# Attention states kept compact: state product in quarters of the array, state update by heads in column halves, y in two banks shared with the scores

One core of one Trainium2 chip runs the whole program. The metric is device time of one execution in microseconds (us); every time here is the median of a kernel's fast runs if nothing else is said. "TensorE" is the matrix engine, "VectorE" the vector engine, "ScalarE" the one for activation functions, "GpSimd" the general engine, "SyncE" the one that issues most of the transfers.

## What is computed

```python
batch, n_heads, seq, head_dim = (4, 8, 768, 64)
for t in range(S):                                   # retention, per batch and head
    state = gamma * state + outer(k[t], v[t])        # 64 x 64
    y[t] = scale * (q[t] @ state)
x = y.transpose(0, 2, 1, 3).reshape(B * S, H * D)    # 3072 x 512
h = x @ w_in                                         # 512 x 2048
g = h * sigmoid(1.702 * h)
out = g @ w_out                                      # 2048 x 512, fp32
```

The kernel does the recurrence by chunks of 128 tokens: 4 sequences of 6 chunks. In a chunk, y is the masked scores times v (the score part) plus q times the state that the chunk found (the state part); then the state is updated with k and v of the chunk. A sequence's first chunk has no state part and its last no update. Four chunks are one block of 512 tokens for the MLP. The weights come as 8-byte numbers and are narrowed to fp32 by VectorE and ScalarE in the first 155 us or so.

## The kernel before

The attention of a chunk, which runs between units of the MLP's matmuls (cuts are marked `# ...`):

```python
y = ps.tile([P, HP, P], F32, name="py", tag="att")          # one bank; pt and pu use the same two buffers
if c:
    for hp in range(HP):                                    # state part: 2 heads at once, block-diagonal 128x128 state
        pe.matmul(y[:, hp, :], old[:, hp, :], qt[:, hp, :], start=(hp == 0), stop=False, ...)
for hp in range(HP):                                        # score part: column halves
    for i in range(2):
        pe.matmul(y[i * D:(i + 1) * D, hp, :], vn[:, 2 * hp + i, :], a[:, i, hp, :], ...)
dve.tensor_mul(x[...], y, rowd)                             # y read out and scaled
# ...
u = ps.tile([P, HP, P], F32, name="pu", tag="att")
for hp in range(HP):                                        # update: 128x128, of which only two 64x64 corners are wanted
    h = slice(2 * hp, 2 * hp + 2)
    pe.matmul(u[:, hp, :], kd[:, h, :]..., vn[:, h, :]..., start=True, stop=True)
for i in range(2):                                          # the two corners, one after the other
    r = slice(i * D, (i + 1) * D)
    # ...
    pool.tensor_mul(new[r, :, r], old[r, :, r], cold[r, 2 * H:, None]...)
    dve.tensor_add(new[r, :, r], new[r, :, r], u[r, :, r])
```

The fetch of a piece of w_in, and what SyncE's queue holds at the start:

```python
w1v = moe_w_in.bitcast(U32).rearrange("(c p) (f two) -> p c f two", p=P, two=2)
# ...
sp.dma_start(x.rearrange("p (c f) two -> p c f two", c=2) if i < NFF else x, SRC[i])   # 512 KB over 128 partitions
# ...
load(0)                    # q, k, v of the first chunk
fetch()
load(1)                    # q, k, v of the second chunk
for _ in range(5):
    fetch()
# ...
turn(0)                    # transposes q and k; then queues q and k of the third chunk, behind the six fetches
```

Of the kernel before, what the change touches and what calls it, by code (L numbers as in the profile page):

```python
# [9 lines left out]
F32 = mybir.dt.float32  # L10
U32 = mybir.dt.uint32
AF = mybir.ActivationFunctionType
ALU = mybir.AluOpType
P = 128
# [14 lines left out]
def kernel(  # L29
# [29 lines left out]
    pe, act, dve, pool, sp = nc.tensor, nc.scalar, nc.vector, nc.gpsimd, nc.sync  # L59
    ctx.enter_context(tc.manual_schedule(engines={mybir.EngineType.PE}))  # L60

    B, H, S, D = q.shape
    NT, DM = out.shape
    DFF = moe_w_in.shape[1]
    HP = H // 2
# [6 lines left out]
    NFF = DFF // P  # L72
    NP = NFF // 2
# [4 lines left out]
    const = ctx.enter_context(tc.tile_pool(name="const", bufs=1))  # L78
    one = ctx.enter_context(tc.tile_pool(name="one", bufs=1))
    two = ctx.enter_context(tc.tile_pool(name="two", bufs=2))  # L80
    ps_a = ctx.enter_context(tc.tile_pool(name="ps_a", bufs=1, space=bass.MemoryType.PSUM))
    ps = ctx.enter_context(tc.tile_pool(name="ps", bufs=2, space=bass.MemoryType.PSUM))
# [13 lines left out]
    rowd = const.tile([P, HP, P], F32, name="rowd")  # L96
    cold = const.tile([P, 2 * H + HP], F32, name="cold")
    ident = const.tile([P, P], F32, name="ident")
    mask = const.tile([P, 2, HP, P], F32, name="mask")
    state = [const.tile([P, HP, P], F32, name=f"state{i}") for i in range(2)]  # L100


    QKV = {}
# [1 line left out]
    def load(j, what="qkv"):  # L105


        b, c = divmod(j, NC)
        rows = slice(c * P, (c + 1) * P)

        def plain(name, src, tag, bufs):
            QKV[name, j] = two.tile([P, H, D], F32, name=name + "_in", tag=tag, bufs=bufs)
            sp.dma_start(QKV[name, j], src[b, :, rows, :].rearrange("h p d -> p h d"))

        if j < 2 * CB:
            if "q" in what:
                plain("q", q, "q_sq", 2)
                plain("kn", k, "k_sq", 2)
        else:
            for name, src in (("q", q), ("k", k)):  # L120
                t = two.tile([P, HP, P // C4, C4], F32, name=name + "_sq")
                for r0 in range(0, P, C4):
                    d0 = r0 % D
                    for hp in range(HP):
                        tc.keep_in_program_order(sp.dma_start(
                            t[r0:r0 + C4, hp],
                            src[b, 2 * hp + r0 // D, rows, d0:d0 + C4].rearrange("(s p) d -> p s d", p=C4)))
                QKV[name, j] = t
            if c < NC - 1:
                plain("kn", k, "kn", 1)  # L130
        if "v" in what:
            plain("v", v, "v", 2)


    w1v = moe_w_in.bitcast(U32).rearrange("(c p) (f two) -> p c f two", p=P, two=2)
    w2v = moe_w_out.bitcast(U32).rearrange("(f p) (e two) -> p f e two", p=P, two=2)
    RAWS = [r.rearrange("p a b -> p (a b)").bitcast(U32)
            for r in (W2[:, 4], W2[:, 5], G[:, 6:8].rearrange("p a s t -> p a (s t)"))]

    SRC = [w1v[:, 2 * h:2 * h + 2, 2 * p * P:2 * (p + 1) * P] for p in range(NP) for h in range(2)] \  # L140
        + [w2v[:, f] for f in range(NFF)]
    fetched = [0]

    def raw(i, n=1):
        x = RAWS[i // 2 % 3]
        return x[:, i % 2 * 1024:(i % 2 + n) * 1024]

    def fetch():
        i = fetched[0]
        if i < len(SRC):  # L150
            x = raw(i).rearrange("p (n two) -> p n two", two=2)
            sp.dma_start(x.rearrange("p (c f) two -> p c f two", c=2) if i < NFF else x, SRC[i])
            fetched[0] = i + 1

    narrowed = [0]
# [1 line left out]
    def narrow():  # L157


        i = narrowed[0]  # L160
        if i == len(SRC):
            return
# [29 lines left out]
        for _ in range(n):  # L192
            fetch()
# [4 lines left out]
    def home(j, name):  # L198

        at = ["qT", "kT", "kd", "at"].index(name)  # L200
        shape = [[HP, P], [HP, P], [H, D], [2, HP, P]][at]
        if j >= 2 * CB:
            return one.tile([P] + shape, F32, name=name, tag=name)
        if at < 3:
            t = G[:, at, j % 2 * 2:j % 2 * 2 + 2]
            return t.rearrange("p s t -> p (s t)").rearrange("p (a b) -> p a b", a=shape[0])
        return G[:, 3 + j % 2].rearrange("p s t -> p (s t)").rearrange("p (a b c) -> p a b c", a=2, b=HP)
# [19 lines left out]
            load(j + 2, "qk" if j + 2 < 2 * CB else "qkv")  # L227

    def attend(j):
        p = ps_a.tile([P, 2, HP, P], F32, name="pa")  # L230
        for hp in range(HP):
            for i in range(2):
                r = slice(i * D, (i + 1) * D)
                pe.matmul(p[:, i, hp, :], KT[j][r, hp, :], QT[j][r, hp, :], start=True, stop=True)  # L234
        AT[j] = home(j, "at")
        for i in range(2):
            dve.tensor_mul(AT[j][:, i], p[:, i], mask[:, i])  # L237
        KT.pop(j)

    def finish(j):  # L240
        c = j % NC
        old, new = state[c % 2], state[(c + 1) % 2]
        vn, a, qt = QKV.pop(("v", j)), AT.pop(j), QT.pop(j)
        y = ps.tile([P, HP, P], F32, name="py", tag="att")
        if c:
            for hp in range(HP):
                pe.matmul(y[:, hp, :], old[:, hp, :], qt[:, hp, :], start=(hp == 0), stop=False,  # L247
                          skip_group_check=True)
        for hp in range(HP):
            for i in range(2):  # L250
                pe.matmul(y[i * D:(i + 1) * D, hp, :], vn[:, 2 * hp + i, :], a[:, i, hp, :],  # L251
                          start=(not c and hp == 0), stop=(hp == HP - 1), skip_group_check=True)
        half, t0 = divmod(j % CB * P, TH)
        x = X1 if j // CB == 1 else X
        dve.tensor_mul(x[:, 2 * half:2 * half + 2, :, t0:t0 + P].rearrange("p s c t -> p (s c) t"), y, rowd)  # L255
        if j + 2 < 2 * CB:
            load(j + 2, "v")
        if c == NC - 1:
            return
        kd = KD.pop(j)  # L260
        u = ps.tile([P, HP, P], F32, name="pu", tag="att")
        for hp in range(HP):
            h = slice(2 * hp, 2 * hp + 2)
            pe.matmul(u[:, hp, :], kd[:, h, :].rearrange("p i d -> p (i d)"),  # L264
                      vn[:, h, :].rearrange("p i d -> p (i d)"), start=True, stop=True)
        for i in range(2):
            r = slice(i * D, (i + 1) * D)
            if c == 0:
                dve.tensor_copy(new[r, :, r], u[r, :, r])  # L269
            else:  # L270
                pool.tensor_mul(new[r, :, r], old[r, :, r],  # L271
                                cold[r, 2 * H:, None].to_broadcast([D, HP, D]))
                dve.tensor_add(new[r, :, r], new[r, :, r], u[r, :, r])


    def hidden(g, h):
# [156 lines left out]


    act.dma_start(cold, col_decay)
    for s in range(2):
        act.dma_start(
            rowd[s * D:(s + 1) * D],
            bass.AP(tensor=row_decay.tensor, offset=row_decay.offset + s * P,
                    ap=[[0, D], [2 * P, HP], [1, P]]),  # L440
        )
    load(0)
    fetch()
    load(1)
    for _ in range(5):
        fetch()
    make_identity(nc, ident)

    for i in range(2):
        for hp in range(HP):  # L450
            h = 2 * hp + i
# [1 line left out]
    m3 = mask.rearrange("s i h t -> s (i h) t")  # L453
    pool.affine_select(out=m3, in_=m3, compare_op=ALU.is_ge, fill=0.0, base=0,
                       pattern=[[0, H], [1, P]], channel_multiplier=-1)

    for t in state:
        dve.memset(t, 0.0)

    def chunks(m):  # L460

        return [s for j in range(m * CB, (m + 1) * CB)
                for s in (lambda j=j: turn(j), lambda j=j: attend(j), lambda j=j: finish(j))]

    turn(0)
    for j in range(CB):
        attend(j)
        narrow()
        turn(j + 1)
        finish(j)  # L470
        if j == 0:
            narrow()
        else:
            up0(0, j - 1)
# [78 lines left out]
```

## Time and profile before

| | before |
|---|---|
| time | 724.99 us (724.62 to 725.17, 3 runs) |
| TensorE busy | 705.4 us, 98% of the span of 722.5 |
| full chunk of attention in the later part, by differences of starts | 3.00 us |
| first matmul of the second block's up-projection | 114.1 us |

The last row splits the run in two. Before 114.1 the weights arrive and are narrowed, and TensorE waits now and then; after it TensorE is hardly ever idle (busy 603.9 of 608.4 us). The 608.4 us from there to the end of the span can be counted in matmuls, the start can't. TensorE's first 30 us:

```profile
11.22 1.09 PE L217 MATMUL pt<-ident,q_in 128*128 128x128 f32 x4 [0.60 <-DMA q_in<-in_q_dram]
...
21.57 1.09 PE L217 MATMUL pt<-ident,q_in 128*128 128x128 f32 x4 [4.41 <-DMA q_in<-in_q_dram]
```

(start, length, engine, line, operation, result and operands, count; in brackets the idle time ahead and what ended it. Of the results, pt is a transpose, pa the scores, py the chunk's y, pu its update, ph the MLP's up-projection and pd its down-projection; G, W and X are buffers that several things share.)

### The profile page before, as it was taken

What the parts mean: (1) busy time and instruction counts of PE and PEld (TensorE: products, weight loads), DVE (VectorE), ACT (ScalarE), POOL (GpSimd) and SP (SyncE); (2) the same over time, 40 slices, a digit from 0 to 9 for tenths busy, and PEclk for the clock granted to TensorE, in tenths of its full rate; (3) what the DMA queues carried; (4) which work ended last, traced back from release to release, by engine and by line L of the source; (5) the groups of instructions that cost most, each with busy time, mean ns of one, the idle gap of its engine ahead of it and who ended that gap; (6) DMA issues with size and microseconds to landing.
All of it is one profiled execution on the core that took longest, in us unless ns stands there. A gap on an engine that the chain in (4) does not pass through costs nothing.

```text
span 722.5 us, 9662 instructions
## 1 busy us (share of the span) xinstructions
PE 705.4 (98%) x3776; PEld 588.5 (81%) x3776; DVE 373.2 (52%) x542; ACT 126.7 (18%) x197; POOL 125.7 (17%) x115
## 2 busy tenths in 40 slices
PE   5799999999999999999999999999999999999997
PEld 4688885447888888888888888888888888888886
DVE  4888889993612822443743353553345373244251
ACT  2313323221000001331000332000233000133100
POOL 2241001000464403000333000123100140200030
PEclk9899999999999999999999999999999999999999
DMA  9995333420012324101334200324300320100001
GB/s 255 232 199 145 132 132 114 147 35 11 15 45 40 73 49 103 31 1 16 74 59 87 59 1 8 73 46 86 67 0 2 63 54 1 44 0 1 15 0 44
DMA packets 142765, 46.28 MB, mean 64 GB/s; under 512 B 129920, under 2 KB 136576, under 8 KB 142720
## 3 DMA queue, kind: packets, MB, share of 16 engines
q1 hardware_dynamic: 135504, 39.10, 23.8%
q10 hardware_dynamic: 7216, 6.57, 2.9%
q8 instruction: 30, 0.49, 0.3%
q14 instruction: 15, 0.12, 0.1%
HBM read 39.33 MB, written 6.29 MB: 63 GB/s over the span
## 4 chain that ended last, share of the span: by engine, by line
PE 92%; DVE 5%; DMA 1%; ACT 1%; issue 0%; SPq 0%; ACTq 0%
PE pd L403 38%; PE px L352 15%; PE py L352 11%; PE ph L313 8%; PE ph L300 7%; PE py L251 3%; PE pa L234 3%; PE pu L264 3%; PE py L247 2%; DMA q_in<-in_q_dram 1%; PE pt L217 1%; DVE W L342 1%; DVE G L342 1%; DVE W L343 1%; DVE G L343 1%; ACT W L181 0%
## 5 line engine op out<-in xcount | busy, mean ns | idle before, releaser
L403 PE MATMUL pd<-W,G 128*128 128x256 f32 x1120 | 250.3, 381 | 0.4 <-DVE G L343 0.3
L403 PEld LDWEIGHTS pd<-W,G 128*128 128x128 f32 x1120 | 210.1, 190 | 30.8 <-DVE G L343 1.2
L352 PE MATMUL px<-X,W 128*128 128x256 f32 x512 | 119.0, 379 | 0.0
L352 PEld LDWEIGHTS px<-X,W 128*128 128x128 f32 x512 | 97.3, 190 | 13.2
L352 PE MATMUL py<-X,W 128*128 128x256 f32 x384 | 90.7, 379 | 0.0
L352 PEld LDWEIGHTS py<-X,W 128*128 128x128 f32 x384 | 73.0, 190 | 9.9
L300 PE MATMUL ph<-X,W 128*128 128x256 f32 x256 | 58.2, 382 | 0.0
L225 POOL TENSOR_TENSOR kd<-kn_in,cold 128x512 f32<-128x512 f32 x13 | 13.6, 1042 | 242.0 <-PE pu L264 199.0
L313 PE MATMUL ph<-W,W 128*128 128x512 f32 x128 | 55.1, 592 | 0.0
L300 PEld LDWEIGHTS ph<-X,W 128*128 128x128 f32 x256 | 47.5, 190 | 6.7 <-DVE X L255 0.2
L313 PEld LDWEIGHTS ph<-W,W 128*128 128x128 f32 x128 | 24.3, 190 | 30.2 <-issue 29.2
L344 POOL TENSOR_TENSOR G<-G 128x512 f32<-128x512 f32 x20 | 28.9, 1444 | 113.1 <-DVE G L343 111.7
L237 DVE TENSOR_TENSOR at<-pa,mask 128x512 f32<-128x512 f32 x32 | 20.6, 684 | 45.5 <-PE pa L234 45.5
L281 DVE TENSOR_TENSOR G<-G,sg 128x512 f32<-128x512 f32 x48 | 33.0, 688 | 13.7 <-ACT sg L279 13.7
L279 ACT ACTIVATE sg<-G 128x512 f32<-128x512 f32 x48 | 30.3, 630 | 50.9 <-DVE G L362 30.6
L279 ACT ACTIVATE sg<-ph 128x512 f32<-128x512 f32 x32 | 19.1, 598 | 104.7 <-PE ph L300 56.2
L403 PE MATMUL pd<-W,W 128*128 128x256 f32 x160 | 35.6, 380 | 0.4 <-DVE W L343 0.3
L403 PEld LDWEIGHTS pd<-W,W 128*128 128x128 f32 x160 | 30.2, 190 | 5.6 <-DVE W L343 1.2
L271 POOL TENSOR_TENSOR state<-state,cold 64x256 f32<-64x256 f32 x32 | 25.6, 800 | 44.0 <-DVE state L269 24.8
L255 DVE TENSOR_TENSOR X<-py,rowd 128x512 f32<-128x512 f32 x20 | 13.8, 688 | 33.3 <-PE py L251 33.3
L390 ACT ACTIVATE u<-pd 128x512 f32<-128x512 f32 x6 | 3.6, 597 | 155.1 <-PE pd L403 155.1
L362 DVE TENSOR_TENSOR G<-py,p 128x512 f32<-128x512 f32 x16 | 11.1, 691 | 37.8 <-PE py L352 37.8
(96 smaller groups left out, 682.1 us busy)
## 6 DMA issues: line engine op xcount, KB each, us to landing
v_in<-in_v_dram SPq DMA_DIRECT2D x24, 256.0 KB, 3.9
W<-in_moe_w_in_dram SPq DMA_DIRECT2D x12, 512.0 KB, 5.1
out_dram<-o ACTq DMA_DIRECT2D x24, 256.0 KB, 2.4
kn_in<-in_k_dram SPq DMA_DIRECT2D x21, 256.0 KB, 4.1
W<-in_moe_w_out_dram SPq DMA_DIRECT2D x10, 512.0 KB, 3.7
q_sq<-in_q_dram SPq DMA_DIRECT2D x256, 16.0 KB, 1.8
k_sq<-in_k_dram SPq DMA_DIRECT2D x256, 16.0 KB, 1.8
G<-in_moe_w_out_dram SPq DMA_DIRECT2D x6, 512.0 KB, 3.8
```

Source lines behind the costliest of these rows:

```text
L234: pe.matmul(p[:, i, hp, :], KT[j][r, hp, :], QT[j][r, hp, :], start=True, stop=True)
L237: dve.tensor_mul(AT[j][:, i], p[:, i], mask[:, i])
L251: pe.matmul(y[i * D:(i + 1) * D, hp, :], vn[:, 2 * hp + i, :], a[:, i, hp, :], start=(not c and hp == 0), stop=(hp == HP - 1), skip_group_ ...
L264: pe.matmul(u[:, hp, :], kd[:, h, :].rearrange("p i d -> p (i d)"), vn[:, h, :].rearrange("p i d -> p (i d)"), start=True, stop=True)
L271: pool.tensor_mul(new[r, :, r], old[r, :, r], cold[r, 2 * H:, None].to_broadcast([D, HP, D]))
L279: act.activation(s, h, AF.Sigmoid, scale=1.702)
L281: dve.tensor_mul(g, h[:, i], s[:, i])
L300: pe.matmul(h[:, ab], w, X[:, 2 * half + c // 2, c % 2, :], start=(ab == 0 and c == 0), stop=(c == 3), skip_group_check=True)
L313: pe.matmul(h, w, X1[:, c // 2:4:2, c % 2, :], start=(c == 0), stop=(c == 3))
L344: pool.tensor_sub(a[1], a[1], a[0])
L352: pe.matmul(acc[:, u, :], W1[:, 2 * d + u, sa, c, :], X[:, sb, c, :], start=(start and u == 0 and c == 0), stop=(stop and c == 1), skip_gr ...
L403: pe.matmul(p0[:, n, :], g1(m, p, sa)[:, n * P:(n + 1) * P], W2[:, sb, p, :], start=(new and p == 0 and n == 0), stop=(last and p == NP - ...
```

## The change

The state of two heads was a 128x128 block of which two 64x64 corners are used, so TensorE multiplied zeros in the state part and computed unwanted corners in the update. Now the state is 64 columns wide: the state part becomes eight 64x64 products on four quarters of the array, the update eight products on column halves with 64 moving columns, and its VectorE and GpSimd work one instruction each. The new y takes the two banks of the scores, in turn with them, one for each row half. That puts other pairs of heads side by side in x, so w_in's rows are permuted to match as they are fetched. Each 512 KB fetch of w_in thereby becomes two, of 64 partitions each.

```diff
-    state = [const.tile([P, HP, P], F32, ...) for i in range(2)]
+    state = [const.tile([P, HP, D], F32, ...) for i in range(2)]
-    w1v = moe_w_in.bitcast(U32).rearrange("(c p) (f two) -> p c f two", p=P, two=2)
+    w1v = moe_w_in.bitcast(U32).rearrange("(o c r d) (f two) -> c r d o f two", o=2, c=2, d=D, two=2)
# ... fetch:
-            sp.dma_start(x.rearrange("p (c f) two -> p c f two", c=2) if i < NFF else x, SRC[i])
+            if i < NFF:
+                for c in range(2):
+                    sp.dma_start(x[c * D:(c + 1) * D].rearrange("p (o f) two -> p o f two", o=2), SRC[i][c])
+            else:
+                sp.dma_start(x, SRC[i])
# ... finish:
-        y = ps.tile([P, HP, P], F32, name="py", tag="att")
+        y = ps_a.tile([P, 2, HP, P], F32, name="py", tag="pa")
+        where = [(y[s % 2 * D:(s % 2 + 1) * D, r, s // 2, :], s, r) for s in range(HP) for r in range(2)]
         if c:
-            for hp in range(HP):
-                pe.matmul(y[:, hp, :], old[:, hp, :], qt[:, hp, :], ...)
+            for out, s, r in where:
+                k = slice(r * D, (r + 1) * D)
+                pe.matmul(out, old[k, s, :], qt[k, s, :], ...)
+        for out, s, r in where:
+            pe.matmul(out, vn[:, 2 * s + r, :], a[:, r, s, :], ...)
# ... the update:
-        u = ps.tile([P, HP, P], F32, name="pu", tag="att")
+        u = ps.tile([P, HP, D], F32, name="pu", tag="att")
+        for s in range(HP):
+            for r in range(2):
+                pe.matmul(u[r * D:(r + 1) * D, s, :], kd[:, 2 * s + r, :], vn[:, 2 * s + r, :], ...)
+        # ... whole-tile copy, or scale and add, in place of two halves
-    for t in state:
-        dve.memset(t, 0.0)
# ... (row decays loaded in the new order of heads)
```

More of the change, by code (lines that the diff above doesn't have):

```diff
@@ L99 @@
     mask = const.tile([P, 2, HP, P], F32, name="mask")
-    state = [const.tile([P, HP, P], F32, name=f"state{i}") for i in range(2)]
+    state = [const.tile([P, HP, D], F32, name=f"state{i}") for i in range(2)]
     QKV = {}
@@ L138 @@
             for r in (W2[:, 4], W2[:, 5], G[:, 6:8].rearrange("p a s t -> p a (s t)"))]
-    SRC = [w1v[:, 2 * h:2 * h + 2, 2 * p * P:2 * (p + 1) * P] for p in range(NP) for h in range(2)] \
+    SRC = [[w1v[c, h, :, :, 2 * p * P:2 * (p + 1) * P] for c in range(2)] for p in range(NP) for h in range(2)] \
         + [w2v[:, f] for f in range(NFF)]
@@ L229, in attend @@
     def attend(j):
-        p = ps_a.tile([P, 2, HP, P], F32, name="pa")
+        p = ps_a.tile([P, 2, HP, P], F32, name="pa", tag="pa")
         for hp in range(HP):
@@ L243, in finish @@
         vn, a, qt = QKV.pop(("v", j)), AT.pop(j), QT.pop(j)
-        y = ps.tile([P, HP, P], F32, name="py", tag="att")
+        y = ps_a.tile([P, 2, HP, P], F32, name="py", tag="pa")
+        where = [(y[s % 2 * D:(s % 2 + 1) * D, r, s // 2, :], s, r) for s in range(HP) for r in range(2)]
         if c:
-            for hp in range(HP):
-                pe.matmul(y[:, hp, :], old[:, hp, :], qt[:, hp, :], start=(hp == 0), stop=False,
-                          skip_group_check=True)
-        for hp in range(HP):
-            for i in range(2):
-                pe.matmul(y[i * D:(i + 1) * D, hp, :], vn[:, 2 * hp + i, :], a[:, i, hp, :],
-                          start=(not c and hp == 0), stop=(hp == HP - 1), skip_group_check=True)
+            for out, s, r in where:
+                k = slice(r * D, (r + 1) * D)
+                pe.matmul(out, old[k, s, :], qt[k, s, :], start=(s < 2), stop=False, skip_group_check=True)
+        for out, s, r in where:
+            pe.matmul(out, vn[:, 2 * s + r, :], a[:, r, s, :], start=(not c and s < 2), stop=(s >= 2),
+                      skip_group_check=True)
         half, t0 = divmod(j % CB * P, TH)
         x = X1 if j // CB == 1 else X
-        dve.tensor_mul(x[:, 2 * half:2 * half + 2, :, t0:t0 + P].rearrange("p s c t -> p (s c) t"), y, rowd)
+        dve.tensor_mul(x[:, 2 * half:2 * half + 2, :, t0:t0 + P], y[:, :, 0:2, :],
+                       rowd.rearrange("p (r o) t -> p r o t", r=2))
         if j + 2 < 2 * CB:
@@ L260, in finish @@
         kd = KD.pop(j)
-        u = ps.tile([P, HP, P], F32, name="pu", tag="att")
-        for hp in range(HP):
-            h = slice(2 * hp, 2 * hp + 2)
-            pe.matmul(u[:, hp, :], kd[:, h, :].rearrange("p i d -> p (i d)"),
-                      vn[:, h, :].rearrange("p i d -> p (i d)"), start=True, stop=True)
-        for i in range(2):
-            r = slice(i * D, (i + 1) * D)
-            if c == 0:
-                dve.tensor_copy(new[r, :, r], u[r, :, r])
-            else:
-                pool.tensor_mul(new[r, :, r], old[r, :, r],
-                                cold[r, 2 * H:, None].to_broadcast([D, HP, D]))
-                dve.tensor_add(new[r, :, r], new[r, :, r], u[r, :, r])
+        u = ps.tile([P, HP, D], F32, name="pu", tag="att")
+        for s in range(HP):
+            for r in range(2):
+                pe.matmul(u[r * D:(r + 1) * D, s, :], kd[:, 2 * s + r, :], vn[:, 2 * s + r, :],
+                          start=(s == 0), stop=True, skip_group_check=True)
+        if c == 0:
+            dve.tensor_copy(new, u)
+        else:
+            pool.tensor_mul(new, old, cold[:, 2 * H:, None].to_broadcast([P, HP, D]))
+            dve.tensor_add(new, new, u)
     def hidden(g, h):
@@ L435 @@
     act.dma_start(cold, col_decay)
-    for s in range(2):
-        act.dma_start(
-            rowd[s * D:(s + 1) * D],
-            bass.AP(tensor=row_decay.tensor, offset=row_decay.offset + s * P,
-                    ap=[[0, D], [2 * P, HP], [1, P]]),
-        )
+    for c in range(2):
+        for r in range(2):
+            act.dma_start(
+                rowd[c * D:(c + 1) * D, 2 * r:2 * r + 2],
+                bass.AP(tensor=row_decay.tensor, offset=row_decay.offset + (2 * c + r) * P,
+                        ap=[[0, D], [4 * P, 2], [1, P]]))
     load(0)
```

## The prediction

> **What bounds the kernel now.** I read the page's busy line and slices first, then the chain that ended last, then one attention chunk in the timeline, then stretches of the start.
>
> ```profile
> PE 705.4 (98%) x3776; PEld 588.5 (81%) x3776; DVE 373.2 (52%) x542; ACT 126.7 (18%) x197; POOL 125.7 (17%) x115
> PE   5799999999999999999999999999999999999997
> DVE  4888889993612822443743353553345373244251
> PE 92%; DVE 5%; DMA 1%; ACT 1%; issue 0%; SPq 0%; ACTq 0%
> PE pd L403 38%; PE px L352 15%; PE py L352 11%; PE ph L313 8%; PE ph L300 7%; PE py L251 3%; PE pa L234 3%; PE pu L264 3%; PE py L247 2%; DMA q_in<-in_q_dram 1%; PE pt L217 1%; DVE W L342 1%; DVE G L342 1%; DVE W L343 1%; DVE G L343 1%; ACT W L181 0%
> ```
>
> TensorE is the bound: 98% busy, all but a few us of its idle time in the first two slices. The changed lines are on the chain with 2% (L247, queries times state), 3% (L251, values times scores) and 3% (L264, the update): about 58 us at most, so only a shorter TensorE program gains. The second row to watch is VectorE, at eight to nine tenths in the first nine slices. A steady chunk (times are starts):
>
> ```profile
> 239.94 1.16 PE L234 MATMUL pa<-qT,kT 64*128 64x128 f32 x16
> ...
> 241.03 3.72 PE L403 MATMUL pd<-W,G 128*128 128x256 f32 x16
> ...
> 243.50 1.28 DVE L237 TENSOR_TENSOR at<-pa,mask 128x512 f32<-128x512 f32 x2
> ...
> 244.59 1.05 PE L247 MATMUL py<-qT,state 128*128 128x128 f32 x8
> ...
> 245.57 1.09 PE L251 MATMUL py<-at,v_in 128*64 128x128 f32 x16
> ...
> 246.59 1.16 PE L264 MATMUL pu<-v_in,kd 128*128 128x128 f32 x8
> ...
> 247.59 2.76 PE L403 MATMUL pd<-W,G 128*128 128x256 f32 x12
> ...
> 249.85 0.68 DVE L255 TENSOR_TENSOR X<-py,rowd 128x512 f32<-128x512 f32 x1
> ```
>
> Every fp32 matmul shows as two records (L247's four as x8), so two passes. Differences of the starts are what TensorE spends: 0.98 us on the state part of y, 1.02 on the score part, 1.00 on the update, 3.00 for a chunk with all three. The state and update matmuls run on the whole array (128*128), the score part in column halves (128*64).
>
> [...]The 16 pd records between pa and L247 take 3.56 us, where the chain gives 16 records without a switch 3.45, so 0.11 is a weight load laid bare. The 32 pd records that run into the next pa take 254.59-247.59 = 7.00 where the chain has 6.91, so 0.09 is the drain. One switch is 0.20 us into 128 columns, about 0.15 into 64. [...]L247 less its drain is 0.89 us for 8 records, 0.112 each. Half-array records run in pairs: the 16 of L251, less 0.09 drain and 0.05 load, take 0.88, so 8 slots of 0.109. [...]
>
> **The change part by part.**
> State part of y: four whole-array matmuls become eight 64x64 ones. They write 16 records, each streaming 128 columns as before, on four tiles. Four at a time is 4 slots of 0.109 = 0.44 us in place of 0.89. It adds a switch before it (0.09 drain; its own load is 0.05) and the one after it now leads from quarters to halves.
> Score part: the same 16 records in 8 slots, 0.88 + 0.05 load. The order is now four passes of one half, then four of the other, where it was two and two.
> Update: four whole-array matmuls become eight column halves with 64 moving columns. [...]So 16 records in 8 slots of about 0.056 are 0.45, for 0.89. It follows the score part in the same mode, so the switch between them (0.20) goes. One is added behind it, back to pd (0.20).
> Sum for a chunk with all three: before 3.00; after 0.09 + (0.05+0.44+0.09) + (0.05+0.88) + 0.45 + (0.09+0.11) = 2.25. Saved 0.75. A sequence's first chunk has no state part: before 0.09+1.02+1.00 = 2.11, after 0.09+0.93+0.45+0.20 = 1.67, saved 0.45 with rounding. Its last has no update: 2.11 against 1.80, saved 0.31. With 4 sequences of 6 chunks: 16 x 0.75 + 4 x 0.45 + 4 x 0.31 = **15.0 us** if nothing waits. Of it 5.0 belong to the eight chunks of the first 115 us, 10.0 to the sixteen after.
>
> What takes some back: y now shares its two banks with the scores. So its first matmul waits until VectorE has read both halves of the scores; before, only the score part needed them, 0.98 us later. In the chunk above the reading ends at 243.50+1.28 = 244.78, 0.19 after y starts at 244.59. Less the 0.09 of drain[...], the wait is about 0.16. The same place in each of the four later blocks (the chunk that meets the sums on VectorE) has this, the other twelve have 2.2 us of slack: -0.65 in all. The other direction is free there: X<-py ends at 250.53, the next scores start at 254.59.
>
> In the start it costs more. Comparing the reading's end with y's start for chunks 2 to 7, chunks 2, 3, 5 and 7 have y 0.13, 0.37, 0.70 and 0.47 ahead of it, so waits of about 0.3, 0.5, 0.7 and 0.4. Chunk 0 gains nothing (TensorE waits for q until 21.6 anyway), chunk 1 part of it:
>
> ```profile
> 20.00:30.00 10.00, 7.92 (x43) 6.38 (x44) 9.25 (x13) 3.40 (x4) 2.02 (x2) 0.66 0.95 214
> 40.00:50.00 10.00, 9.69 (x78) 8.24 (x77) 9.84 (x13) 2.75 (x4) 4.24 (x4) 1.00 0.86 206
> 90.00:114.00 24.00, 24.00 (x158) 21.05 (x155) 21.98 (x31) 5.84 (x9) 3.85 (x4) 1.00 0.34 110
> ```
>
> (columns: PE, PEld, DVE, ACT, POOL busy us with counts, clock, DMA share, GB/s). With VectorE at 9.25, 9.84 of 10 and 21.98 of 24 us, and DMA at 0.95, TensorE can't run far ahead. Of the 5.0 us I keep 2.
>
> Off the path: the state updates on 64x256 halves (VectorE about 0.42 us, twice a chunk) become one on 128x256, so VectorE loses some 0.4 us a chunk, and GpSimd half its state instructions; both only help the start. The two memsets (0.5 us each) lay before the first data. The q and k transposes no longer share their two buffers with y; that removes waits of 0.3 to 0.5 us of L247 on ScalarE in chunks 1 to 3, which the new wait replaces. Sixteen w_in fetches become thirty-two of half size, and SyncE needs some 0.4 us for each more, on a stretch where DMA is full: up to 0.5 us lost.
>
> Net: 10.0 - 0.65 + 2 - 0.5 = about 11 us, if the array packs as hoped.
>
> **The rivals.**
> (a) Quarters don't run four at a time, only two. For: nothing in this trace shows more than two tiles at once, and two passes of one tile stand next to each other. Against: pairs already overtake a waiting pass[...]. Then the state part is 0.88 instead of 0.44, costing 0.44 x 20 = 8.8 us: about 722.5.
> (b) The new order of the score part, four passes of one half in a row, is longer than the look-ahead. One slot lost per chunk is 0.109 x 24 = 2.6 us, two 5.2. For: no place in the trace has such a run. Against: in pairs the second tile starts as if the first's queue were not there. About 716.5 to 719.
> (c) The new wait on VectorE eats all the start's gain and more: the start then gives 0, about 716.
> (d) Everything packs and the start gains its whole 5 us, as VectorE is relieved: about 711.
>
> **Range and chances.** Full packing gives 725.0 - 11 = 714. I give (a) one in six, some of (b) one in three, and (d) one in five; these about cancel around the middle, so I say 714.0 us, with 709.5 to 721 to hold it 8 times in 10. A gain over 2% needs 14.5 us, nearly all of the 15.0 without a wait: 0.15. Slower by 2% would need the change to cost more than every gain, and I see no wait of that size: 0.02. The rest, 0.83, is within 2%.
>
> **What would show it right or wrong.** In the timeline of a late chunk: the state part's 16 records 0.58 us from the first start to the score part's (1.0 means rival a); the score part to the update 0.93 (1.04 or more means b); the update to pd about 0.54. A full chunk is 2.25 us instead of 3.00. TensorE idle before the state part, put down to VectorE's scores line, should be 0.1 to 0.2 us in four late chunks and 0.3 to 0.7 in some early ones. The third part, the up-projection of the second block, should start about 2 us before its 114.1. I am wrong if the late chunks save nothing, or if the first 115 us grow.

What is cut from this text are rules and figures that no trace of this case shows: on changes of shape, on weight loads, on the order of matmuls, on banks, on the split of a transfer, on tiles, and an allowance of time for VectorE's signal. Its sum came to 10.0 - 0.65 + 2 - 0.5 = about 11 us. The 0.65 is four waits of 0.16, of which 0.19 - 0.09 = 0.10 each comes from the trace and the rest is the allowance. The 0.5 for the split fetch stands on SyncE's records (q's at 0.80 and 20.07 us take 0.44 and 0.42); that the halves themselves would be no slower was not measured.

"Drain" and "load" are names for times that the trace of before shows at a change of shape; what the array does in them it doesn't show. Within L247's run and within L251's, a pass follows on the one before it (in L251 a pair on a pair) after 0.11 us. Into the score part it is 0.20 (245.37, 245.57), so 0.09 more, and to its second pair 0.16 (245.73), so 0.05 more; into the update it is 0.20 (246.39, 246.59) and to its second pass 0.21 (246.81), 0.10 more. The weight loads' records take 190 ns for 128 columns (update) and 136 for 64 (score part). The slot of 0.056 in the update is an estimate, half of the 0.112 between L247's records. "Look-ahead" is the word for how many waiting passes of one tile a pass of another can overtake. That they overtake is in the trace: all of L251's 16 records start in pairs less than 0.01 us apart, the first pair included (245.57, 245.58), though the program has the two passes of one half next to each other.

## More of the kernel before

TensorE transposes the second chunk's q at 11.22 and the third chunk's at 21.57, and waits 4.41 us for the latter to arrive. What the transfers do meanwhile, by stretches:

```profile
12.00:16.00 4.00, 3.90 (x30) 3.01 (x28) 3.28 (x6) 1.87 (x3) 1.04 (x1) 1.00 1.05 362
16.00:20.00 4.00, 1.17 (x17) 0.97 (x16) 3.86 (x8) 0.00 (x0) 2.04 (x2) 1.00 1.10 357
```

(busy us and counts of TensorE, its weight loads, VectorE, ScalarE, GpSimd; granted clock; share of the DMA engines; GB/s moved.) The last two columns count: the DMA engines are full, and while w_in's rows of 2 KB arrive, full means some 360 GB/s. (In the 4 us before, which bring mostly the short rows of q, k and v, they are as full and move 254.)

## The result

The changed kernel takes 719.56 us (718.91 to 720.40, 4 runs) where the kernel before took 725.08 beside it (4 runs): ratio 0.9919, 95% interval 0.9899 to 0.9940, so some 5.9 us faster. Ratios here are the mean time of one kernel's fast runs over that of the other's of the same rounds, so they differ a little from the ratio of the medians. A second submission of the same file gave 0.9909 (0.9895 to 0.9923).

The changed kernel's busy times and its first slices:

```profile
PE 693.1 (97%) x4096; PEld 572.5 (80%) x4096; DVE 362.6 (51%) x520; ACT 126.8 (18%) x197; POOL 111.2 (15%) x99
...
PE   5599999999999999999999999999999999999997
...
DVE  2787898995512742444643444463345373244251
```

TensorE is busy 12.3 us less than before, but the span shrank by only 4.8 (722.5 to 717.7): the rest became idle time. The second slice of TensorE fell from 7 to 5, and VectorE's first slices from 4, 8, 8, 8, 8 to 2, 7, 8, 7, 8. Nearly all of that is in the start. A late chunk of the changed kernel, the counterpart of the chunk in the prediction (one of the four in which VectorE is busy with sums for the MLP):

```profile
243.26 3.72 PE L408 MATMUL pd<-W,G 128*128 128x256 f32 x16
247.16 0.67 PE L256 MATMUL py<-qT,state 64*64 64x128 f32 x16 [0.18 <-DVE at L242]
247.75 1.15 PE L258 MATMUL py<-at,v_in 128*64 128x128 f32 x16
248.68 0.69 PE L272 MATMUL pu<-v_in,kd 128*64 128x64 f32 x16
249.29 0.92 PE L408 MATMUL pd<-W,G 128*128 128x256 f32 x3
```

By differences of starts the state part takes 0.60 us instead of 0.98, the score part 0.92 instead of 1.02, the update 0.61 instead of 1.00: four 64x64 tiles do run at once (in this chunk four of the state part's records start within 0.02 us, from 247.155 to 247.175). From the first pd record ahead of it to the state part it is 3.90 here, against 3.65 in a chunk without a wait, so the new wait on VectorE costs 0.25, of which the trace shows 0.18 as idle. The start, in contrast:

```profile
12.30 1.09 PE L222 MATMUL pt<-ident,q_in 128*128 128x128 f32 x4 [2.37 <-DMA q_in<-in_q_dram]
...
27.08 1.12 PE L222 MATMUL pt<-ident,q_in 128*128 128x128 f32 x4 [8.29 <-DMA q_in<-in_q_dram]
```

The third chunk's q is there 5.5 us later than before; TensorE waits 8.29 us for it instead of 4.41. The stretches show why: the DMA engines are as full as before and move a third less.

```profile
12.00:16.00 4.00, 3.58 (x22) 2.92 (x24) 1.29 (x3) 1.19 (x2) 1.04 (x1) 1.00 1.14 227
16.00:20.00 4.00, 2.77 (x38) 2.42 (x34) 3.38 (x7) 0.67 (x1) 0.99 (x1) 1.00 1.07 242
```

In the trace of before, whole 512 KB fetches land 1.40 us apart (14.64, 16.10, 17.44, 18.81, 20.23 us); in the changed kernel halves land 1.08 apart (16.09, 17.17, 18.25, 19.33), so 2.16 for the same bytes. Six fetches lie ahead of the third chunk's q: 6 x 0.76 = 4.6 of the 5.5 us.

The late arrival goes with a lower clock, too. The third number from the end is TensorE's granted clock; first the line of before, then that of the changed kernel:

```profile
28.00:32.00 4.00, 3.99 (x24) 3.35 (x21) 3.15 (x5) 0.00 (x0) 2.53 (x3) 0.99 0.18 43
28.00:32.00 4.00, 3.36 (x31) 2.54 (x32) 3.05 (x2) 2.48 (x3) 1.15 (x1) 0.50 1.26 219
```

The clock is 0.50 for 6.8 us of before's start, for 13.7 of the changed kernel's and for 10.2 in the trace of its second submission. If half of TensorE's busy time in these stretches counts as lost (my estimate), that is 3.0, 3.6 and 2.7 us. The last two belong to the same kernel, and their starts differ by 1.0 us; so a start in a single trace is good to about 1 us, and smaller differences of starts below prove nothing.

And the first up-projection of the second block, the border between the two parts:

```profile
L318 PE MATMUL ph<-W,W x128: 592/592/593, 117.0 to 171.5; 128*128 128x512 f32 x128
```

(durations min/median/max, first and last start.) It starts 2.9 us later than the 114.1 of before (1.9 in the trace of the second submission, 116.0). From there to the end it is 717.7 - 117.0 = 600.7 us, where before took 608.4. So the late part gained 7.7 and the start lost 2.9; 4.8 is what the spans show.

### The profile page after: what moved, and what is told of

Same layout as the page of the kernel before. It is cut to its first block, busy times and chain, and to the rows that moved or that the text cites. A ratio compares the mean times of both kernels' runs of the same rounds, so it can differ in the third digit from the quotient of the medians.

```text
span 717.7 us, 10277 instructions
## 1 busy us (share of the span) xinstructions
PE 693.1 (97%) x4096; PEld 572.5 (80%) x4096; DVE 362.6 (51%) x520; ACT 126.8 (18%) x197; POOL 111.2 (15%) x99
## 4 chain that ended last, share of the span: by engine, by line
PE 76%; DVE 10%; SPq 6%; DMA 4%; issue 2%; ACT 1%; ACTq 0%; DVEq 0%
PE pd L408 29%; PE px L357 15%; PE py L357 12%; PE ph L318 8%; SPq L125 5%; PE ph L305 5%; PE py L258 3%; DVE G L347 2%; PE pa L239 2%; PE py L256 2%; DMA kn_in<-in_k_dram 1%; DVE G L348 1%; DVE G L346 1%; PE pu L272 1%; DMA W<-in_moe_w_in_dram 1%
## 5 line engine op out<-in xcount | busy, mean ns | idle before, releaser
L286 DVE TENSOR_TENSOR G<-G,sg 128x512 f32<-128x512 f32 x48 | 33.1, 689 | 13.7 <-ACT sg L284 13.7
L262 DVE TENSOR_TENSOR X<-py,rowd 128x512 f32<-128x512 f32 x20 | 13.7, 687 | 36.3 <-PE py L258 36.3
L381 DVE TENSOR_TENSOR G<-py,vv 128x512 f32<-128x512 f32 x16 | 11.1, 692 | 25.4 <-ACT vv L378 25.4
```

The source lines that it names most:

```text
L286: dve.tensor_mul(g, h[:, i], s[:, i])
```

## Experiments

My theory: the late part is the predicted packing, with small terms off, and the start is lost to the fetch in partition halves alone. Rivals: (1) it is the number of transfers, not where they go; (2) it is the shared banks, y waiting on VectorE's reading of the scores; (3) the new order of the passes loses slots. All twelve runs gave correct results.

### split_part and split_col: the fetch alone

Both are the kernel before, with each w_in fetch made two of 256 KB. The first splits by partitions, as the change does; the second by columns, each half still over all 128 partitions. Count, size and length of the rows (2 KB) are the same.

```diff
+                y = x.rearrange("p (c f) two -> p c f two", c=2)
+                for u in range(2):
+                    sp.dma_start(y[u * D:(u + 1) * D], SRC[i][u * D:(u + 1) * D])     # split_part
+                    sp.dma_start(y[:, u], SRC[i][:, u])                               # split_col
```

> The kernel before, with one thing of the change: each w_in fetch as two transfers of 256 KB, one to partitions 0 to 63 and one to 64 to 127. Theory A (a transfer into 64 partitions runs at about two thirds of the rate, so the first 50 us wait for data): landings of the halves about 1.08 us apart, q of the third chunk in at about 26 instead of 21.4 us, time 728.5 to 731 against 725. Theory B (twice as many transfers cost, whatever their shape): the same. Theory C (the start was lost to y waiting for the scores in the shared banks): 725, no change.

> The kernel before, each w_in fetch again as two transfers of 256 KB of the same 2 KB rows, but each into all 128 partitions (one of the two channel blocks). Theory A: landings about 0.7 us apart, time within 0.2% of 725. Theory B: as the split by partitions, 728.5 to 731. Theory C: 725.

Measured: split_part 729.88 us, ratio 1.0068 (1.0056 to 1.0080), which is 4.9 us slower; split_col 724.30, ratio 1.0002 (0.9988 to 1.0015). The stretches of split_part:

```profile
12.00:16.00 4.00, 3.60 (x22) 2.92 (x24) 1.27 (x3) 1.20 (x2) 1.04 (x1) 1.00 1.08 224
16.00:20.00 4.00, 3.62 (x30) 2.87 (x26) 2.46 (x5) 0.67 (x1) 0.97 (x1) 1.00 1.07 237
```

and of split_col:

```profile
12.00:16.00 4.00, 3.99 (x28) 3.33 (x28) 2.88 (x5) 1.76 (x3) 0.98 (x1) 1.00 1.03 361
16.00:20.00 4.00, 1.28 (x18) 0.97 (x16) 3.76 (x8) 0.00 (x0) 2.04 (x2) 1.00 1.10 350
```

Full engines move some 230 GB/s into 64 partitions and some 355 into 128. Split_part's up-projection of the second block shows the whole loss ahead of it:

```profile
L318 PE MATMUL ph<-W,W x128: 592/592/593, 118.5 to 173.0; 128*128 128x512 f32 x128
```

118.5 is 4.4 later than before, and from there to the end split_part takes 608.4 us, the same as before; split_col starts it at 114.2. So rival (1) is out: twice the transfers cost nothing, and the narrow reach of each costs 4.4 us in the trace, 4.9 by the ratio. As split_part keeps y in its own bank, rival (2) isn't needed for the loss either. The changed kernel starts the up-projection 1.5 us before split_part (2.5 in its second trace), which is what the rest of the change gains in the start.

Why fetches into one half of the partitions are slow, no run shows; the runs show only that they are: halves of 256 KB, in turn to either side, land 1.08 us apart, which is 243 GB/s, where fetches into all 128 move some 360. Such halves also read other rows of w_in than whole fetches do. No run separates this, but the halves of split_part and of the changed kernel read different rows and land at nearly the same pace, 1.09 and 1.08 us apart.

### heads and heads2: the change without the split

If the two heads of a pair are taken from the two halves of the heads (head 4r + s in place of 2s + r), x comes out in w_in's natural order and the fetch can stay whole. The transposes must then pair other heads. In "heads" they became plain products with the identity, by column halves; "heads2" keeps the whole-array transposes and brings q and k of the first eight chunks in two transfers each that interleave the heads, over all partitions.

```diff
+    def head(s, r):
+        return 4 * r + s
-            pe.matmul(out, vn[:, 2 * s + r, :], a[:, r, s, :], ...)
+            pe.matmul(out, vn[:, head(s, r), :], a[:, r, s, :], ...)
# w1v, SRC and fetch as in the kernel before
-                for hp in range(HP):
-                    pe.transpose(p[:, hp, :], x[:, 2 * hp:2 * hp + 2, :]..., ident)
+                for s in range(HP):                              # heads
+                    for r in range(2):
+                        pe.matmul(p[r * D:(r + 1) * D, s, :], x[:, head(s, r), :], ident, ...)
-            sp.dma_start(QKV[name, j], src[b, :, rows, :]...)
+                for r in range(2):                               # heads2, which keeps pe.transpose
+                    sp.dma_start(t[:, r::2, :], x[:, HP * r:HP * (r + 1), :])
```

> The changed kernel with heads placed so that X keeps its order of channels of before: slot s, row half r holds head 4r+s (it was 2s+r). w_in is then fetched whole again and the row decays in two transfers; the eight early transposes go head by head in column halves. Quarters, update and shared banks stay. Theories A and B: the third chunk's q lands near 21.5 again, the late chunks stay at 2.23 us, time 712 to 715. Theory C: the start stays 3 us late, about 719 to 720.

> As heads, but the early transposes are whole-array ones again, 8 records for the two where heads took 32 (0.87 us against 1.90 in its trace, and two switches more); instead q and k of the first eight chunks come in two transfers each, all into 128 partitions. If the half-partition fetch is what held the change (theory A), the third chunk starts near 21.6 us, the second block's up-projection about 111 to 112 us (before 114.1, the change 117.0), time 712 to 714. If more transfers in the start cost by their number after all (theory B), or the shared banks do (theory C), 717 or more.

Measured: heads 717.16 us, 0.9895 (0.9882 to 0.9908); heads2 715.91, 0.9870 (0.9848 to 0.9891), so 9.4 us faster than before. Both miss what theory A said (712 to 715 and 712 to 714). "Heads" removed the late arrival (its third chunk's q lands at 22.09 us, before at 21.44, changed 27.03) and yet won little: its up-projection began at 115.2. Its trace shows a cost that I had put in myself:

```profile
64.66 1.09 PE L222 MATMUL pt<-ident,q_in 128*64 128x128 f32 x16
65.58 1.04 PE L222 MATMUL pt<-ident,kn_in 128*64 128x128 f32 x16
66.56 1.78 PE L305 MATMUL ph<-X,W 128*128 128x256 f32 x7
```

The q and k transposes take 66.56 - 64.66 = 1.90 us in 32 records; as whole-array transposes they are 8 records in 0.88 (below). That is 1.02 us more in each chunk where TensorE transposes, the eight early ones. Heads2 has 8 records again:

```profile
65.49 0.60 PE L226 MATMUL pt<-ident,q_in 128*128 128x128 f32 x4
65.93 0.60 PE L226 MATMUL pt<-ident,kn_in 128*128 128x128 f32 x4
66.37 1.89 PE L314 MATMUL ph<-X,W 128*128 128x256 f32 x8
```

and starts the up-projection at 113.5, which is 0.6 before the kernel before and 3.5 before the changed one. Its late part takes 600.5 us, as the changed kernel's 600.7. So the fetch held back most of what the change lost, but its removal did not give the start the 1.5 us or more that the comparison with split_part promised; heads2 isn't a clean removal, since eight chunks have two more transfers and GpSimd scales their k in another order of heads. Its trace has one wait of 3.21 us at 30.00, until VectorE, which was narrowing weights, had read y of the second chunk; "best" (below), whose early chunks differ only in the order of the score part, waits 0.78 us there and begins at 111.5.

### update_alone and quarters_alone: the two gains by themselves

The first is the kernel before with only the update in column halves, into the corners of the old 128x128 state; the second the changed kernel with the old whole-array update.

```diff
# update_alone, on the kernel before
-            pe.matmul(u[:, hp, :], kd[:, h, :]..., vn[:, h, :]..., start=True, stop=True)
+            for i in range(2):
+                r = slice(i * D, (i + 1) * D)
+                pe.matmul(u[r, hp, r], kd[:, 2 * hp + i, :], vn[:, 2 * hp + i, :], ...)
# quarters_alone, on the changed kernel: the old update's four products, its two corners read out one by one
```

> The kernel before with only the update in column halves (states still block-diagonal, y as before in its own bank, fetch as before). My sum by parts: before 0.09+1.00, after 0.61+0.11, so 0.37 us for each of 20 updates, of which the 13 late ones count in full: 4.8 us, the 7 early ones in part: 718.5 to 720.5. If instead the late gain of the change needs its parts together, 724 to 725.

> The changed kernel with the update on the whole array again (four 128x128 matmuls, the diagonal blocks read from them); the quarters, the shared banks and the split fetch stay. By parts, with the durations of the traces: after y 0.09 drain, 1.00 of the update, nothing after; in the change 0.61 and 0.11. So 0.37 for each of 20 updates: 719.6 + 5 to 7.5 = 724.5 to 727. If quarters and update gain only together, more than 728.

Measured: update_alone 717.14 us, 0.9896 (0.9883 to 0.9908), 7.5 us faster, more than the 718.5 to 720.5 that I expected and no less than the whole change (0.9919 and 0.9909, with intervals that overlap); quarters_alone 726.67, 1.0017 (0.9995 to 1.0039). Late chunks of update_alone:

```profile
243.34 1.09 PE L251 MATMUL py<-at,v_in 128*64 128x128 f32 x16
244.26 0.64 PE L265 MATMUL pu<-v_in,kd 128*64 128x64 f32 x16
244.83 1.35 PE L404 MATMUL pd<-W,G 128*128 128x256 f32 x5
```

and of quarters_alone:

```profile
249.48 0.67 PE L256 MATMUL py<-qT,state 64*64 64x128 f32 x16 [0.18 <-DVE at L242]
250.08 1.15 PE L258 MATMUL py<-at,v_in 128*64 128x128 f32 x16
251.15 1.16 PE L272 MATMUL pu<-v_in,kd 128*128 128x128 f32 x8
252.15 1.03 PE L411 MATMUL pd<-W,G 128*128 128x256 f32 x4
```

The update in halves costs 0.57 and lets the score part end without a change of shape (0.92 instead of 1.02): from 608.4 the late part falls to 715.2 - 112.3 = 602.9, a gain of 5.5. The quarters save 0.38 in the state part, lose 0.05 in the score part, have an added switch, and wait in the same four chunks (0.18 idle above): 725.2 - 118.9 = 606.3, a gain of 2.1. The two sum to 7.6, and the changed kernel's is 7.7. So the parts add up in the late part, the update is nearly three quarters of the gain, and the quarters, alone, don't pay for the split fetch that came with them (the up-projection starts at 118.9); heads2 shows that they can do without it.

### y_own: y out of the shared banks

The changed kernel, with y in the two one-bank buffers that pt and pu use, so that it no longer waits for the scores to be read.

```diff
-        y = ps_a.tile([P, 2, HP, P], F32, name="py", tag="pa")
+        y = [ps.tile([P, HP, P], F32, name="py", tag="att") for _ in range(2)]
# and y's read-out in two instructions, one for each bank
```

> The changed kernel with y in two tiles of the two one-bank buffers, not in the scores' banks. The wait of y for the scores' reading should go: the pd stretch before the state part in the chunk that meets the sums 3.65 us instead of 3.90, the same in four blocks, 1.0 us in all, and two waits of 0.5 us in the first stage. If that sharing is a main cost (theory C) the time falls to 717 or less. My expectation: the update must now wait until y is read out, about 0.7 us in each of 20 chunks and 4 us where VectorE is behind, so 730 to 745.

Measured: 759.40 us, 1.0468 (1.0445 to 1.0491), 34 us slower, beyond the 730 to 745 expected.

```profile
263.61 1.14 PE L258 MATMUL py<-at,v_in 128*64 128x128 f32 x16
268.74 1.12 PE L272 MATMUL pu<-v_in,kd 128*64 128x64 f32 x16 [3.99 <-DVE X L263]
269.79 9.68 PE L408 MATMUL pd<-W,G 128*128 128x256 f32 x32
```

The wait for the scores is gone and a larger one stands in its place: y holds both buffers, so the update has none until VectorE has read y. From score part to update it is 1.71 us in a usual chunk instead of 0.92, and 5.13 in this one, where VectorE is behind. The waits are not all of it: the 32 pd records after this one take 9.61 us instead of 7.10, at a clock of 0.83 from 260 to 280 us. In the whole run the clock is 0.50 for 37 us, worth some 15 us by the estimate above. As a test of rival (2) this is poor, because it moved the wait instead of taking it away. It does show that the shared banks are the cheap choice: in the changed kernel they cost 0.25 us in each of four late chunks, and in the start four waits of 0.43 to 0.63. What TensorE's work on y waited for there (us in total, times), the start first:

```profile
DVE G L242: 2.1, 4
DVE at L242: 0.7, 4
```

### long_runs and alternate: the order of the passes

Both are the changed kernel with another order of the eight products. In the change, two products of one column half (four passes) follow one another; in long_runs four products (eight passes), in alternate one (two passes; score part only).

```diff
-... for s in range(HP) for r in range(2)]
+... for s in (0, 2, 1, 3) for r in range(2)]                          # long_runs
-        for out, s, r in where:
+        for out, s, r in [where[n] for n in (0, 2, 1, 3, 4, 6, 5, 7)]:  # alternate, score part
```

> The changed kernel with y's matmuls in the order s = 0, 2, 1, 3: all of one column half, then all of the other; the score part has eight passes of one half in a row (it has four). If TensorE looks ahead over everything that is queued, the score part stays at 0.92 us and the state part at 0.60. If its look-ahead ends within such a run (rival b of the prediction), they grow by a few slots of 0.109: score part 1.25 to 1.7.

> The changed kernel with the score part's matmuls alternating between the column halves (two passes of one half in a row, as in the kernel before, where the change has four). long_runs has shown that eight passes in a row cost 0.44 us a chunk. If four are still within the look-ahead, the score part stays at 0.92 us; if four already cost something that I took for stream time, it falls below 0.92 (0.81 with one slot less).

Each had one run only, of unknown state (729.11 and 716.98 us), so only the durations in the traces count. A late chunk of long_runs:

```profile
236.05 1.25 PE L258 MATMUL py<-at,v_in 128*64 128x128 f32 x13
237.04 0.27 PE L272 MATMUL pu<-v_in,kd 128*64 128x64 f32 x1
237.14 0.27 PE L258 MATMUL py<-at,v_in 128*64 128x128 f32 x1
...
237.36 0.73 PE L272 MATMUL pu<-v_in,kd 128*64 128x64 f32 x13
238.03 1.35 PE L408 MATMUL pd<-W,G 128*128 128x256 f32 x5
```

and of alternate:

```profile
245.96 1.09 PE L258 MATMUL py<-at,v_in 128*64 128x128 f32 x16
246.88 0.64 PE L272 MATMUL pu<-v_in,kd 128*64 128x64 f32 x16
247.44 0.92 PE L408 MATMUL pd<-W,G 128*128 128x256 f32 x3
```

From the first score pass to pd, long_runs takes 1.98 us, the change 1.54, alternate 1.48. (In alternate the score part stays at 0.92, as expected if four passes are within the look-ahead; the 0.05 comes off the update behind it, 0.56 instead of 0.61.) So the second half's passes do overtake waiting passes of the first, since they start in pairs from the first on (beside the prediction), and 16 passes in strict order of start would not fit into 8 slots; and the reach of that is limited: eight passes of one half in a row lose 0.44 us, four slots of 0.109 (a slot is the time of one pass of 128 columns), and four in a row 0.05. In long_runs the update's first record even starts among the last passes of the score part. What sets that reach, and how many waiting passes it spans, no run here settles. Rival (3) is true in the small: 0.05 us a chunk, about 1 us in all, and in the late part alternate takes 715.1 - 115.3 = 599.8 us, 0.9 less than the change.

### update_first and best: putting it together

Update_first is heads2 with the update ahead of y in every chunk, then the score part, then the state part, so that VectorE has 0.5 us more to read the scores before y needs them. Best does that in the late chunks alone, keeps the old order in the eight early ones, and alternates the halves. A third kernel of the same round was the changed kernel again, for comparison.

```diff
+        if c < NC - 1:                       # best: and j >= 2 * CB
+            # update: its eight products, ahead of y
-        # state part (start=s < 2), then score part
+        # score part (start=s < 2), then state part (start=False)
```

> heads2 with TensorE's order in a chunk turned round: the update first, then the score part, then the state part. The update needs nothing of the scores, so its 0.52 us of passes should cover y's wait for the shared banks: the 3.90 us pd stretch before y back to 3.65 and the two waits of 0.5 us in the first stage gone, 2 us in all; the number of mode switches is the same. 713 to 714.5 if that wait is real time on the path; 715.5 to 716.5 (as heads2) if it is not.

> The change itself once more, on this chip and in these rounds, to set the others against: ratio to the kernel before 0.990 to 0.994.

> heads2 with the two small gains that the traces have shown put together: the score part alternating between column halves (0.05 us in each of 24 chunks, from alternate) in all chunks, and the update first in the sixteen late chunks alone (four waits of 0.25 us, from update_first; its start was slower, so the early chunks keep the old order). 715.9 less 2.2: 713 to 715, ratio to the kernel before 0.983 to 0.986. If these gains are lost in how the first 50 us fall out from build to build, 715 to 717.

Measured: update_first 716.78 us, 0.9886 (0.9873 to 0.9900), above both of its ranges; the changed kernel again 718.25, 0.9909; best 712.76 (712.38 to 714.41, 5 runs), 0.9833 (0.9816 to 0.9850), 12.1 us faster than before. A late chunk of best:

```profile
241.34 0.69 PE L268 MATMUL pu<-v_in,kd 128*64 128x64 f32 x16
241.85 1.05 PE L277 MATMUL py<-at,v_in 128*64 128x128 f32 x16
242.83 0.67 PE L283 MATMUL py<-qT,state 64*64 64x128 f32 x16
...
```

No wait stands there any more. Update_first's late part takes 599.8 us against heads2's 600.5, so 0.7 of the waits' 4 x 0.25 = 1.0 came back; best's takes 710.8 - 111.5 = 599.3, 0.5 less again, where alternating should give 16 x 0.05 = 0.8. Best's border:

```profile
L347 PE MATMUL ph<-W,W x128: 592/592/592, 111.5 to 166.0; 128*128 128x512 f32 x128
```

Update_first's up-projection began at 115.3, though it differs from heads2 (113.5) only in the order within a chunk. Its trace shows no longer waits: TensorE is idle for 17.3 us of the start, in heads2 for 18.2. But the clock is 0.50 for 10.2 us of it against 3.4, by the estimate above a loss of 4.4 us against 1.7. That fits the 1.8 us; why the slow stretch is longer, no run shows. Best, with the old order there, began at 111.5.

## Why the prediction was right in its verdict and short in its size

It said 714.0 us within 709.5 to 721; the result was 719.56, in the range and "within 2%" as thought most likely. Step by step:

- **Packing in the late chunks: right.** Predicted from the start of one part to the next 0.58 (state), 0.93 (score), 0.54 (update); measured 0.60, 0.92, 0.61. Rival (a), two quarters at a time, would have left the state part at 1.0 (and 714 + 8.8 is 722.8, not 722.5). A full chunk with its switches is 0.09 + 0.60 + 0.92 + 0.61 + 0.10 = 2.33, not 2.25, so it saves 0.67.
- **Rival (b), a run longer than the look-ahead: right in kind, half as large as its smallest case.** 0.05 us a chunk, not 0.11. By the prediction's own sign (1.04 or more from score part to update) it stayed away; it hides in the update, of whose excess it is the most: alternated, the update takes 0.56.
- **Waits on VectorE in four late chunks: right place, larger.** The idle time is 0.18, within the 0.1 to 0.2 that it named as a sign, but by differences of starts the cost is 0.25, not 0.16 (its allowance for the signal had no measurement behind it; in the changed kernel 0.16 us lie between the end of VectorE's reading, 245.72 + 1.28 = 247.00, and y's first record at 247.16). With the update's excess this makes the late part's gain 7.7 instead of 10.0 - 0.65 = 9.35.
- **The start keeps 2 us of its gain: about right.** The changed kernel against split_part, which has the same narrow transfers, gains 1.5 to 2.5; update_alone gained 1.8 and best 2.6 against before. Its four waits all came, in chunks 2, 3, 5 and 7: 0.58, 0.63, 0.43 and 0.44 us, 2.1 together where it had 1.9. Rival (c), that these waits eat the start, isn't what happened. (VectorE's "eight to nine tenths in the first nine slices" is a misreading: its first slice is a 4.)
- **"Sixteen w_in fetches become thirty-two of half size, and SyncE needs some 0.4 us for each more ... up to 0.5 us lost": the mis-sized term.** I counted issues and took it, with no trace to show it, that two halves move as fast as the whole. Split_part measured 4.4 to 4.9 us, and split_col that SyncE's share of it is none. In the traces the sum is: predicted 11, gained 4.8 by the spans, so 6.2 missing; 4.4 - 0.5 = 3.9 of them are this term, 1.65 the late part, 0.5 the start.

The border at 114.1 was to come about 2 us earlier; it came 2.9 later. So the time lay in the range partly by luck: its upper half was there for rivals (a) and (b), which took nothing or little, and what filled it was a loss that none of the rivals named. The prediction named exactly this growth of the start ("or if the first 115 us grow") as what would make it wrong, and that check was the one that pointed there. With the fetch whole and the two smaller terms mended, "best" takes 712.76 us, a little under the prediction.

## What to carry to other kernels

When a change permutes data, price the transfers of the permutation by the partitions that each one reaches, not by their number: here fetches over half the partitions took half as long again per byte (2.16 us for 512 KB instead of 1.40), and that stood in the one stage where transfers set the pace. Where a change has parts, ask which part forces the expensive side effect: here the update alone gave three quarters of the late gain without touching the weights. And when half-array products are ordered, try alternating the halves: here that saved 0.05 us a chunk against four passes of one half in a row, and eight in a row lost 0.44.
